# Halving the angle tables of a fused Fourier and mixer kernel's setup, VectorE and ScalarE in step, with masks and identity moved behind the first half

## The chip, the cores and the metric

The kernel runs on one core of a Trainium2 chip. The metric is the device time of one execution in microseconds (us). On one core most executions of the kernel before take 594.2 to 594.5 us. A profile is one execution, and its span is about 1.8 us shorter than the time quoted for it.

TensorE does the matmuls (its weight loads, PEld, run beside them), VectorE (DVE) and ScalarE (ACT) the elementwise work, GpSimd (POOL) issues the loads, SyncE (SP) most of the stores of the result.

## The reference

```python
def reference(x, w_tok1, w_tok2, w_ch1, w_ch2):        # x: 8 x 3008 x 256
    x = fft(fft(x, axis=1), axis=2).real               # Fourier mixing
    h = maximum(x.transpose(0, 2, 1) @ w_tok1, 0) @ w_tok2     # token MLP, 256 hidden
    u = x + h.transpose(0, 2, 1)
    return u + maximum(u @ w_ch1, 0) @ w_ch2           # channel MLP, 1536 hidden
```

## The kernel before

The Fourier transform over 3008 = 64 x 47 positions is made of matmuls with small tables of cosines. The kernel computes these tables itself, in its first 20 us: angles (`mp`), their rounding to whole turns (`vp`), the sine by ScalarE (`tp`, `tq`), then a turn of both tables by TensorE (`pt`, copied to `tt`) and a reversal of their rows with an anti-diagonal matrix (`turn_rows`, `pr`). Meanwhile the first batch is loaded, folded (`xp`), transformed (`pz` to `z`, `pw` to `w`), and carried through the token MLP (`ph`, `pu`, `ut`). At 32 us the first matmul of the channel MLP (`pc`) begins, and from there TensorE works without a pause for 556 us.

The parts that the change touches, cut:

```python
    # head of VectorE
    ts(gt32[:], scol[:], 32.0, AT.is_gt)
    ts(eq32[:], scol[:], 32.0, AT.is_equal)
    ts(mid[:], scol[:], 32.0, AT.is_lt)
    ts(tmp[:], scol[:], 1.0, AT.is_ge)
    nc.vector.tensor_tensor(out=mid[:], in0=mid[:], in1=tmp[:], op=AT.mult)
    # ... reff, offp, gp
    nc.vector.scalar_tensor_tensor(out=mp[:], ...)          # all 12 groups at once
    # ...
    near(vp, mp)                                            # two ScalarE passes of 768
    # ... the small table of z: m1, reduced, sin, t0h
    rest_of(vp, mp, S)
    table3(tp, vp)                                          # two ScalarE passes of 768
    ts(ident[:], jrow[:, 0:P], pcol[:], AT.is_equal)
    # ... vq, anti, t1n, t1b, cfeat/ixc, md

    # the order in which the work is emitted
    warm(24)                            # 24 matmuls that only keep TensorE busy
    table3(tq, vq, (shift0[:], shift1[:]))
    turned_out(tts_p, turn_in(tp, ps_mm))
    filler(12)                          # the same, 128 columns each
    pts_q = turn_in(tq, ps_out)
    filler(4)
    table_d()
    pieces = fold0(); take(pieces, 5)
    own = zw0();      take(own, 2)
    turn_rows(tts_p, 1.0, 0)
    take(own, 3); table_b(); take(own, 3)
    turned_out(tts_q, pts_q)
    # ... three copies of hp, table_perm
    take(own, 4)
    turn_rows(tts_q, -1.0, 0)
    take(own, 3)
    # ...
```

The last batch's result goes out in stores that SP issues, with ScalarE's help, as the last matmuls finish:

```python
                eng = nc.scalar if i and final else nc.sync
                eng.dma_start(
                    out=dram(out_t, (b * S + 8 * c + i + 2 * first) * D,
                             [[NQ * D, 64], [2 * D, nk - first], [1, D]]),
                    in_=osb[64 * i:64 * i + 64, first:nk, :])
```

## Time and profile before

| | kernel before |
|---|---|
| time, median of 3 runs | 594.2 us (594.19 to 594.73) |
| span of the profiled run | 592.44 us |
| TensorE busy | 98% of the span |
| first W product (`pw`) | 18.92 us |
| first matmul of the channel MLP (`pc`) | 32.17 us |
| last TensorE matmul ends | 588.52 us |
| last store landed | 591.14 us |

The lines that carry the prediction are shown in it. How to read them: the page's digits are busy tenths of 40 equal slices; a line of waits gives the engine, what it waited with, what released it, the total in us, how often, and the longest; a line of the chain of waits gives start, length and the work that ended last; a line of the timeline gives start, busy time, engine, source line, operation, tiles out<-in, shapes, count, and in brackets the idle time before it with its releaser.

### The profile page before, as it was taken

To read this page: it belongs to the slowest core of one execution; us is meant where nothing else is said; L and a number is where in the kernel's file an instruction comes from. 1 tells how busy PE (TensorE), PEld (TensorE's weight loads), DVE (VectorE), ACT (ScalarE), POOL (GpSimd) and SP (SyncE) were. 2 spreads that over 40 slices of the span, in tenths; PEclk is the share of its full clock that TensorE was granted. 3 is DMA by queue.
4 is the path that set the end of the run, shared out by engine and by line. 5 is a ranking of instruction groups with operands and counts; after the bars stand their busy time and mean duration, and the time that the engine had idled before them with its cause. 6 is when DMAs were issued, how large, how long until landed. Compare 5 with 4: busy or idle time off the path is not lost.

```text
span 592.4 us, 15959 instructions
## 1 busy us (share of the span) xinstructions
PE 580.4 (98%) x6397; PEld 419.8 (71%) x6397; DVE 458.7 (77%) x1075; ACT 437.7 (74%) x994; POOL 152.7 (26%) x251
## 2 busy tenths in 40 slices
PE   5999999999999999999999999999999999999997
PEld 4846777767776777676777667767777777866676
DVE  8868689878896887769797787868888677676573
ACT  7775887887778777777767776777777867766772
POOL 7530421412151211421134111421211121112131
PEclk9999999999999999999999999999999999999999
DMA  9996851863367242844329432492233335333424
GB/s 151 211 187 126 139 101 46 150 122 54 66 122 139 55 88 56 157 71 98 64 49 170 98 65 55 90 172 54 56 76 63 78 55 97 48 72 72 82 58 105
DMA packets 86683, 56.55 MB, mean 95 GB/s; under 512 B 54945, under 2 KB 83553, under 8 KB 85857
## 3 DMA queue, kind: packets, MB, share of 16 engines
q1 hardware_dynamic: 77984, 37.77, 33.6%
q0 software_dynamic: 8320, 17.49, 17.2%
q8 instruction: 50, 0.82, 0.6%
q10 hardware_dynamic: 304, 0.26, 0.2%
q14 instruction: 25, 0.20, 0.1%
HBM read 34.98 MB, written 24.64 MB: 101 GB/s over the span
## 4 chain that ended last, share of the span: by engine, by line
PE 96%; DVE 2%; ACT 1%; issue 0%; POOL 0%; DVEq 0%; POOLq 0%
PE pc L773 41%; PE px L817 25%; PE py L817 10%; PE pu L730 7%; PE pt L613 4%; PE po L888 2%; PE pz L518 2%; PE pq L645 1%; PE py L645 1%; PE py L836 1%; PE pw L596 1%; PE pw L597 1%; PE pw L560 0%; ACT z L307 0%; PE ph L430 0%; PE ph L432 0%
## 5 line engine op out<-in xcount | busy, mean ns | idle before, releaser
L776 ACT ACTIVATE c<-pc 128x512 f16<-128x512 f32 (+1 forms) x574 | 297.9, 595 | 31.3 <-PE pc L773 16.3
L799 POOL TENSOR_TENSOR osb<-osb,rt 128x256 f32<-128x256 f32 (+1 forms) x92 | 84.5, 919 | 373.3 <-DVE osb L799 366.1
L817 PEld LDWEIGHTS <-c 128*128 128x128 f16 x2112 | 128.1, 98 | 24.9
L773 PE MATMUL pc<-ut,wc1p 128*128 128x512 f16 x576 | 140.0, 379 | 0.5 <-DVE ut L305 0.5
L773 PE MATMUL pc<-ut,wc1m 128*128 128x512 f16 (+1 forms) x576 | 134.9, 370 | 0.0
L822 ACT ACTIVATE m<-px 128x256 f32<-128x256 f32 (+1 forms) x138 | 51.8, 375 | 75.4 <-PE px L817 46.0
L817 PEld LDWEIGHTS <-sb 128*128 128x128 f16 x1584 | 94.6, 98 | 10.4
L738 DVE TENSOR_TENSOR ut<-pu,yt 128x512 f16<-128x512 f32 (+1 forms) x94 | 63.3, 674 | 40.6 <-PE pu L730 40.3
L773 PEld LDWEIGHTS <-wc1p 128*128 128x128 f16 x576 | 52.0, 97 | 49.2 <-DMA wc1p<-in_moe_w_ch_dram,ixc 0.8
L773 PEld LDWEIGHTS <-wc1m 128*128 128x128 f16 x576 | 52.9, 98 | 45.0
L817 PE MATMUL px<-wst,c 128*128 128x128 f16 x1056 | 74.0, 219 | 0.0
L817 PE MATMUL px<-wc,c 128*128 128x128 f16 x1056 | 66.5, 219 | 0.0
L799 DVE TENSOR_TENSOR osb<-py,m 128x256 f32<-128x256 f32 (+1 forms) x92 | 37.5, 407 | 26.5 <-ACT m L822 26.2
L790 DVE TENSOR_TENSOR sb<-sb,c 128x768 f16<-128x768 f16 (+1 forms) x92 | 54.2, 589 | 3.2
L730 PE MATMUL pu<-w2p,uu 128*128 128x512 f16 (+1 forms) x184 | 54.7, 379 | 0.0
L790 DVE TENSOR_TENSOR sb<-c 128x768 f16<-128x768 f16 (+1 forms) x92 | 50.6, 550 | 0.0
L790 DVE TENSOR_TENSOR c<-c 128x768 f16<-128x768 f16 (+1 forms) x92 | 50.5, 548 | 0.0
L790 DVE TENSOR_TENSOR sb<-c,sb 128x768 f16<-128x768 f16 (+1 forms) x92 | 50.4, 548 | 0.0
L307 ACT ACTIVATE z<-pz 128x480 f16<-128x480 f32 (+1 forms) x60 | 39.0, 666 | 5.4 <-PE pz L527 3.0
L599 DVE SCALAR_TENSOR_TENSOR w<-alt,pw 128x131 f16<-128x131 f16 x84 | 29.2, 351 | 16.5 <-ACT w L307 16.0
L652 DVE TENSOR_TENSOR yt<-py,qs 128x512 f16<-128x512 f32 x48 | 30.9, 685 | 10.5 <-ACT qs L648 10.2
L817 PE MATMUL py<-wst,sb 128*128 128x128 f16 x528 | 37.1, 219 | 0.0
(201 smaller groups left out, 648.1 us busy)
## 6 DMA issues: line engine op xcount, KB each, us to landing
out_dram<-osb SPq DMA_DIRECT2D x83, 256.0 KB, 3.8
xp<-in_x_dram POOLq DMA_DIRECT2D x16, 272.0 KB, 5.3
out_dram<-osb SPq DMA_DIRECT2D x11, 192.0 KB, 3.1
xp<-in_x_dram POOLq DMA_DIRECT2D x16, 127.5 KB, 5.8
rt<-ut SPq DMA_TRANSPOSE x96, 3.8
w2s<-in_moe_w_tok_dram POOLq DMA_DIRECT2D x1, 1504.0 KB, 14.8
w1p<-in_moe_w_tok_dram POOLq DMA_DIRECT2D x4, 192.0 KB, 7.9
wc<-in_moe_w_ch_dram POOLq DMA_DIRECT2D x1, 768.0 KB, 15.2
```

The lines of the kernel that those rows point to most:

```text
L307: nc.scalar.activation(out=out_, in_=in_, func=AFT.Copy)
L599: nc.vector.scalar_tensor_tensor(out=w[:, g, 0:131], in0=alt[:], scalar=pw[:, 131:132], in1=pw[:, 0:131], op0=AT.mult, op1=AT.add)
L613: nc.tensor.matmul(pt[:, o:o + n], lhsT=hw[:, g, th * P:th * P + P], rhs=w[:, g, f:f + n], start=(g == 0), stop=(g == NG - 1))
L652: nc.vector.tensor_tensor(out=yt[:, h, CW * c:CW * c + CW], in0=py[:], in1=qs[:], op=op)
L730: nc.tensor.matmul(pu[:, 0:n], lhsT=uu[:, th, int(minus), h, :], rhs=w2_cols(b, c)[:, th], start=(th == 0), stop=(th == 1))
L738: nc.vector.tensor_tensor(out=ut[:, h, 0:n].rearrange("p (a b) -> p a b", b=64), in0=pu[:, 0:n].rearrange("p (b a) -> p a b", b=64), in1=y ...
L773: nc.tensor.matmul(pc[:, 0:n], lhsT=wc[:, h, ct * P:(ct + 1) * P], rhs=ut[:, h, 0:n], start=(h == 0), stop=(h == 1))
L776: nc.scalar.activation(out=c1[:, ct, 0:n], in_=pc[:, 0:n], func=AFT.Relu)
L790: nc.vector.tensor_tensor(out=o, in0=x, in1=y, op=op)
L799: eng.tensor_tensor(out=o, in0=x, in1=y, op=AT.add)
L817: nc.tensor.matmul(o[:, t], lhsT=a(k)[:, f:f + P], rhs=w(k), start=(first and t == 0 and k == 0), stop=(k == HC - 1), skip_group_check=True)
L822: nc.scalar.activation(out=m[:, i, t1], in_=pa[:, 0], func=AFT.Copy)
```

## The change

Its intent: the chain that ends last in the setup goes through one large VectorE instruction, two large ScalarE passes, another VectorE one, and so on, each waiting for the whole of the one before. In halves of six groups the two engines can work side by side. Work that is not needed early (the masks `mid`, the small table of z, the identity) moves behind the first half; the turned rows of p move ahead of the z products; the index of the gathered weights is made by GpSimd. The diff's core, cut:

```diff
-    ts(mid[:], scol[:], 32.0, AT.is_lt)
-    ts(tmp[:], scol[:], 1.0, AT.is_ge)
-    nc.vector.tensor_tensor(out=mid[:], in0=mid[:], in1=tmp[:], op=AT.mult)
...
+    halves = slice(0, NG // 2), slice(NG // 2, NG)
+    for g in halves:
+        nc.vector.scalar_tensor_tensor(out=mp[:, g], ...)
+    ts(mid[:], ...)                       # the three of mid, moved here
+    for g in halves:
+        for i, scale, bias in ((mp, 1.0 / S, up), (vp, 1.0, down)):
+            nc.scalar.activation(out=vp[:, g], in_=i[:, g], func=AFT.Identity,
+                                 scale=scale, bias=bias[:])
+    rest_of(halves[0])
     half = pvec("half0"), pvec("half1")
     ...
+    rest_of(halves[1])
+    ident = const.tile([P, P], FP16, tag="ident")
+    ts(ident[:], jrow[:, 0:P], pcol[:], AT.is_equal)
     quart, side, shift0, shift1 = ...
+    for g in halves:
+        table3(tp, vp, g)
...
-    cfeat = pvec("cfeat")                 # three VectorE instructions for ixc
+        iota(ixc[:], [[0, 1]], D, -1)     # by GpSimd
...
-    Z0_ORDER = ((11, (0, 0)), (0, (1, 1)), (6, (0, 1)), (1, (0, 1)))
+    Z0_ORDER = ((11, (0, 1)), (0, (1, 1)), (6, (0, 1)), (1, (0, 1)))
...
-    warm(24)
-    table3(tq, vq, (shift0[:], shift1[:]))
-    turned_out(tts_p, turn_in(tp, ps_mm))
-    filler(12)
+    warm(12)
+    pts_p = turn_in(tp, ps_mm)
+    turned_out(tts_p, pts_p, (0,))
+    angles_z()
+    turned_out(tts_p, pts_p, (1,))
+    table_q()
+    table_anti()
+    table_z()
+    filler(6)
+    turn_rows(tts_p, 1.0, 0)
+    filler(10)
     pts_q = turn_in(tq, ps_out)
     filler(4)
...
```

Note the fillers. Before there are 24 + 12 + 4 = 40 matmuls that compute nothing, after it 12 + 6 + 10 + 4 = 32. Each comes with a weight load, so TensorE has 16 instructions fewer, and all else it does is the same.

More of the change, by code (lines that the diff above doesn't have):

```diff
@@ L248, in sin, with table3 @@
         nc.scalar.activation(out=out_, in_=in_, func=AFT.Sin, scale=PI2 / period)
-    def table3(tab, r, shift=(0.0, 0.0)):
+    def table3(tab, r, g, shift=(0.0, 0.0)):
         for i in range(2):
-            nc.scalar.activation(out=tab[:, :, 64 * i:64 * i + 64], in_=r[:],
+            nc.scalar.activation(out=tab[:, g, 64 * i:64 * i + 64], in_=r[:, g],
                                  func=AFT.Sin, scale=half[i][:], bias=shift[i])
@@ L268, in turn_in, with turned_out @@
         return pts
-    def turned_out(tts, pts):
-        for h in range(2):
+    def turned_out(tts, pts, hs=(0, 1)):
+        for h in hs:
             copy(0, tts[0][:, 768 * h:768 * h + 768], pts[h][:, 0:768])
@@ L318 @@
     ts(gp[:], jrow[:, 0:NG], r2[:], AT.mult, offp[:], AT.add)
-    nc.vector.scalar_tensor_tensor(
-        out=mp[:], in0=jrow[:, 0:64].unsqueeze(1).to_broadcast([P, NG, 64]),
-        scalar=r47[:], in1=gp[:].unsqueeze(2).to_broadcast([P, NG, 64]),
-        op0=AT.mult, op1=AT.add)
+    halves = slice(0, NG // 2), slice(NG // 2, NG)
+    for g in halves:
+        nc.vector.scalar_tensor_tensor(
+            out=mp[:, g], in0=jrow[:, 0:64].unsqueeze(1).to_broadcast([P, NG // 2, 64]),
+            scalar=r47[:], in1=gp[:, g].unsqueeze(2).to_broadcast([P, NG // 2, 64]),
+            op0=AT.mult, op1=AT.add)
+    ts(mid[:], scol[:], 32.0, AT.is_lt)
+    ts(tmp[:], scol[:], 1.0, AT.is_ge)
+    nc.vector.tensor_tensor(out=mid[:], in0=mid[:], in1=tmp[:], op=AT.mult)
     nc.vector.memset(altu[:], 1.0)
@@ L325, with rest_of @@
         nc.vector.memset(altu[:, f:f + 127:2], -1.0)
-    def near(v, m):
-        for i, scale, bias in ((m, 1.0 / S, up), (v, 1.0, down)):
-            nc.scalar.activation(out=v[:], in_=i[:], func=AFT.Identity, scale=scale,
-                                 bias=bias[:])
-    def rest_of(v, m, period):
-        nc.vector.scalar_tensor_tensor(out=v[:], in0=v[:], scalar=-float(period),
-                                       in1=m[:], op0=AT.mult, op1=AT.add)
-    near(vp, mp)
+    for g in halves:
+        for i, scale, bias in ((mp, 1.0 / S, up), (vp, 1.0, down)):
+            nc.scalar.activation(out=vp[:, g], in_=i[:, g], func=AFT.Identity,
+                                 scale=scale, bias=bias[:])
+    def rest_of(g):
+        nc.vector.scalar_tensor_tensor(out=vp[:, g], in0=vp[:, g], scalar=-float(S),
+                                       in1=mp[:, g], op0=AT.mult, op1=AT.add)
+    rest_of(halves[0])
     half = pvec("half0"), pvec("half1")
@@ L345, with table_q, table_anti @@
                                        op0=AT.mult, op1=AT.mult)
+    for g in halves:
+        table3(tp, vp, g)
+    anti = const.tile([P, P], FP16, tag="anti")
+    acol = pvec("acol")
+    def table_q():
+        for g in halves:
+            nc.vector.scalar_tensor_tensor(out=vq[:, g], in0=vp[:, g], scalar=side[:],
+                                           in1=vp[:, g], op0=AT.mult, op1=AT.max)
+        for g in halves:
+            table3(tq, vq, g, (shift0[:], shift1[:]))
+    def table_anti():
+        ts(acol[:], pcol[:], -1.0, AT.mult, 127.0, AT.add)
+        ts(anti[:], jrow[:, 0:P], acol[:], AT.is_equal)
     mask0, mask0h, q24 = (pvec(n) for n in ("mask0", "mask0h", "q24"))
-    ts(mask0h[:], xicol[:], -0.5, AT.mult, 0.5, AT.add)
-    ts(q24[:], qcol[:], 24.0, AT.add)
     t1n = const.tile([KR, 2, 2, 24], FP16, tag="t1n")
@@ L351 @@
     m1 = gen.tile([KR, 5, 24], FP32, tag="m1")
-    for a, n, col, off in ((0, 2, qcol, 47 / 4), (2, 2, qcol, 0.0), (4, 1, q24, 47 / 8)):
-        ts(m1[:, a:a + n, :], jrow[0:KR, 0:24].unsqueeze(1).to_broadcast([KR, n, 24]),
-           col[0:KR, :], AT.mult, off, AT.add)
     cs, v1 = (gen.tile([KR, 5, 24], FP32, tag=n, name=n) for n in ("cs", "v1"))
-    reduced(v1[:], m1[:], m1[:], 47)
-    sin(cs[:], m1[:], 47)
     t0h = gen.tile([KR, 2, 24], FP16, tag="t0h")
-    nc.scalar.activation(out=t0h[:], in_=cs[:, 0:4:2, :], func=AFT.Copy,
-                         scale=mask0h[0:KR, :])
@@ L361 @@
-    rest_of(vp, mp, S)
-    table3(tp, vp)
-    ident = const.tile([P, P], FP16, tag="ident")
-    ts(ident[:], jrow[:, 0:P], pcol[:], AT.is_equal)
-    nc.vector.scalar_tensor_tensor(out=vq[:], in0=vp[:], scalar=side[:], in1=vp[:],
-                                   op0=AT.mult, op1=AT.max)
-    anti = const.tile([P, P], FP16, tag="anti")
-    acol = pvec("acol")
-    ts(acol[:], pcol[:], -1.0, AT.mult, 127.0, AT.add)
-    ts(anti[:], jrow[:, 0:P], acol[:], AT.is_equal)
-    ts(mask0[:], mask0h[:], 2.0, AT.mult)
@@ L372, with angles_z @@
-    for i, m in ((0, mask0), (1, xicol)):
-        ts(t1n[:, :, i, :], cs[:, i:4:2, :], m[0:KR, :], AT.mult)
-    ts(t1b[:, 1, :], cs[:, 4, :], float(np.sqrt(0.5)), AT.mult,
-       xicol[0:KR, :], AT.mult)
-    nc.vector.tensor_copy(out=t1b[:, 0:3:2, :], in_=t1n[:, :, 0, :])
+    def angles_z():
+        ts(mask0h[:], xicol[:], -0.5, AT.mult, 0.5, AT.add)
+        ts(q24[:], qcol[:], 24.0, AT.add)
+        for a, n, col, off in ((0, 2, qcol, 47 / 4), (2, 2, qcol, 0.0),
+                               (4, 1, q24, 47 / 8)):
+            ts(m1[:, a:a + n, :], jrow[0:KR, 0:24].unsqueeze(1).to_broadcast([KR, n, 24]),
+               col[0:KR, :], AT.mult, off, AT.add)
+        reduced(v1[:], m1[:], m1[:], 47)
+        sin(cs[:], m1[:], 47)
+        nc.scalar.activation(out=t0h[:], in_=cs[:, 0:4:2, :], func=AFT.Copy,
+                             scale=mask0h[0:KR, :])
@@ L377, with table_z @@
+    def table_z():
+        ts(mask0[:], mask0h[:], 2.0, AT.mult)
+        for i, m in ((0, mask0), (1, xicol)):
+            ts(t1n[:, :, i, :], cs[:, i:4:2, :], m[0:KR, :], AT.mult)
+        ts(t1b[:, 1, :], cs[:, 4, :], float(np.sqrt(0.5)), AT.mult,
+           xicol[0:KR, :], AT.mult)
+        nc.vector.tensor_copy(out=t1b[:, 0:3:2, :], in_=t1n[:, :, 0, :])
     nyq = const.tile([KR, P], FP16, tag="nyq")
     ixc = const.tile([P, 1], I32, tag="ixc")
-    cfeat = pvec("cfeat")
-    ts(cfeat[:], pcol[:], 1.0, AT.is_lt, -128.0, AT.mult)
@@ L381, with rows_c, angles_d @@
-    ts(cfeat[:], cfeat[:], 256.0, AT.add)
-    nc.vector.tensor_tensor(out=ixc[:], in0=cfeat[:], in1=pcol[:], op=AT.subtract)
-    nc.vector.scalar_tensor_tensor(out=md[:], in0=vd[:], scalar=-256.0, in1=md[:],
-                                   op0=AT.mult, op1=AT.add)
+    def rows_c():
+        iota(ixc[:], [[0, 1]], D, -1)
+        pl.memset(ixc[0:1, :], P)
+        load_wc()
+    def angles_d():
+        nc.vector.scalar_tensor_tensor(out=md[:], in0=vd[:], scalar=-256.0, in1=md[:],
+                                       op0=AT.mult, op1=AT.add)
@@ L387 @@
     alt = const.tile([P, 131], FP16, tag="alt")
-    load_wc()
     def table_d():
@@ L932, in take @@
             next(g, None)
-    warm(24)
-    table3(tq, vq, (shift0[:], shift1[:]))
+    warm(12)
     held.add("o2")
-    turned_out(tts_p, turn_in(tp, ps_mm))
-    filler(12)
+    pts_p = turn_in(tp, ps_mm)
[8 more added lines that the diff above has]
+    filler(10)
     pts_q = turn_in(tq, ps_out)
     filler(4)
-    table_d()
+    rows_c()
     pieces = fold0()
-    take(pieces, 5)
+    take(pieces, 2)
+    angles_d()
+    take(pieces, 3)
     own = zw0()
     take(own, 2)
-    turn_rows(tts_p, 1.0, 0)
+    turned_out(tts_q, pts_q, (0,))
     take(own, 3)
+    turned_out(tts_q, pts_q, (1,))
+    held.clear()
+    take(own, 3)
+    table_d()
     table_b()
-    take(own, 3)
-    turned_out(tts_q, pts_q)
-    held.clear()
-    for g2, e in enumerate((1, 1, 0)):
-        carried(tts_p, hp, g2, e)
+    carried(tts_p, hp, 0, 0)
+    carried(tts_p, hp, 1, 1)
+    turn_rows(tts_q, -1.0, 0)
+    carried(tts_p, hp, 2, 1)
     table_perm()
-    take(own, 4)
-    turn_rows(tts_q, -1.0, 0)
-    take(own, 3)
+    take(own, 7)
     carried(tts_p, hp, 3, 1)
```

## The prediction

> **What bounds the kernel now.** I read the page first, for the share of each engine and the clock:
>
> ```profile
> PE 580.4 (98%) x6397; PEld 419.8 (71%) x6397; DVE 458.7 (77%) x1075; ACT 437.7 (74%) x994; POOL 152.7 (26%) x251
> ...
> PE   5999999999999999999999999999999999999997
> ...
> PE 96%; DVE 2%; ACT 1%; issue 0%; POOL 0%; DVEq 0%; POOLq 0%
> ```
>
> TensorE is the bound, and the only slice with room is the first (its digit is 5). The whole table of waits of TensorE over the span says the same:
>
> ```profile
> PE filler L294 <- DVE altu L325: 5.9, 1, 5.9
> PE pz L518 <- ACT tt L287: 0.6, 1, 0.6
> PE pc L773 <- DVE ut L305: 0.5, 1, 0.5
> PE pw L560 <- ACT tt L307: 0.4, 1, 0.4
> PE pz L518 <- DVE xp L488: 0.4, 1, 0.4
> PE pt L265 <- ACT tq L252: 0.3, 1, 0.3
> ```
>
> All six fall before 32.2 us. From the first matmul of the first MLP layer (`pc`) to the end, TensorE never waits. The matmuls after it are the same in both kernels, so the question is only: at what time does that first `pc` start? The chain of waits, cut to its first 42 us, shows who sets that time (start, length, what):
>
> ```profile
> 4.26 1.02 DVE mp L319
> ...
> 8.09 0.87 DVE vp L333
> ...
> 12.16 0.77 DVE xp L488 x2
> ...
> 14.50 1.08 ACT z L307 x2
> 15.58 1.45 ACT tt L287 x3
> ...
> 18.92 1.09 PE pw L560 x16
> ```
>
> VectorE leads up to 13.4 us almost without a hole, ScalarE from 14.5 to 18.9, then TensorE is fed back to back from 18.92 to about 31.4. That is the chain which the change works on. But there is a second arm, which the chain does not show because it ended a tenth of a microsecond earlier. The weight loads' waits and the timeline around 32 us:
>
> ```profile
> PEld L773 <- DMA wc1p<-in_moe_w_ch_dram,ixc: 0.8, 1, 0.8
> ...
> 31.42 0.69 DVE L305 CAST ut<-pu 128x512 f16<-128x512 f32 x1 [1.16 <-PE pu L716]
> ...
> 32.17 1.46 PE L773 MATMUL pc<-ut,wc1p 128*128 128x512 f16 x6 [0.52 <-DVE ut L305]
> ```
>
> and the DMA issue of the same weights, from the timeline and from the list of issues:
>
> ```profile
> 15.79 1.05 POOL L153 DMA_INDIRECT wc1p<-in_moe_w_ch_dram,ixc  x1 [0.96 <-DVE xp L488]
> ...
> wc1p<-in_moe_w_ch_dram,ixc POOLq DMA_INDIRECT x1, 16.2
> ```
>
> 15.79 + 16.2 = 31.99 us: the gathered half of the first layer's weights lands at 31.99, and the weight loads wait for it. `ut`, the end of the compute chain, is there at 31.42 + 0.69 = 32.11. So two arms end within 0.12 us of one another. The second matmul of `pc` (start 32.38 in the trace) is the first that needs the gathered half. The DMA view has the engines at 9 tenths in nearly every slice from 4 us on, at some 195 to 215 GB/s; landings come in the order of issue (w1 by 20.26, w2s 28.21, the direct half of the weights 30.07, the gathered half 31.99). That arm is bandwidth and order, not issue: the gather lay 16 us in the queue.
>
> **What the Trainium skill says.** "DMA: Bandwidth & Descriptors", section "Issuing engines are not separate DMA queues", and the skill's main page "Trainium Kernel Development and Optimization", Key Constraints: all queues share the same 16 DMA engines. Here one queue carries nearly everything, and the trace agrees: an earlier issue behind a full queue gains nothing by itself. "ScalarE: Activation LUTs", section "What ACT_TABLE_LOAD costs": an ACTIVATE costs a fixed part plus 0.833 ns per element. The trace agrees: 255 elements took 0.507 us and 768 took 0.936, so 0.836 ns per element and 0.29 us fixed; that fixed part, less some overlap, is what each split pays. "TensorE: Matmul & The Clock Gate", Part 1: the array runs at half rate until some 3.4 us of sustained activity. The trace agrees: the fillers of 256 columns start at 5.89 and stand 0.213 us apart, and the spacing falls only at about 10.5 us; the transposes of 128 columns from 10.9 on stand 0.056 us apart.
>
> **The change, part by part.** The order of the instructions on each engine in both programs was compared, since the engines run in order.
>
> *The head of VectorE.* The three `mid` instructions leave the head; `reff` starts after `gt`/`eq`, 0.26 us earlier (2.58 for 2.84), so `mp` may start at 4.01. Halved, it takes about 0.59 us a half (estimate: 1.02 less 384 elements at the 0.99 ns per element that the 259- and 512-wide casts, 0.42 and 0.67 us, give, and with overlap), so ScalarE starts on `vp` at 4.60 instead of 5.32: 0.7 us earlier.
>
> *ScalarE.* The rounding is four passes of 384 at about 0.615 us (0.29 + 384 x 0.836 ns) in sequence with two overlaps of 0.1: 4.60 to 7.03, against 7.22 before. `sin`/`t0h` of the small table (0.3 + 0.34) no longer stand ahead of the `tp` table, and `tp` starts at about 6.95 and not 8.99. Its four passes end near 9.1 instead of 10.75: 1.6 us earlier. Then TensorE turns `tp`: the 12 warm matmuls end at 5.89 + 12 x 0.213 = 8.45, the transposes run at half rate (12 x 0.107 = 1.3 us), so the last is in at about 9.9, and `tt` follows half by half, ending near 11.4 instead of 13.98. `tq` (four passes, about 0.6 us apart) then ends near 13.7; it ended at 12.59 before: later, by design. `turn_rows` of p moves ahead to about 13.7-15.3 from 15.47-17.04.
>
> *VectorE up to the fold.* Gone: three `cfeat`/`ixc` instructions (0.45 us; made by GpSimd now). Moved behind the fold's first pieces: `md` (0.42). Added: three splits, about 0.12 us each, and a new idle of about 0.5 us, as the second half of `rest_of` needs ScalarE's fourth pass (7.03) while VectorE is free at 6.6. Saved at the head, after moving `mid` back in: nothing. Net: the fold starts at about 12.3 (12.16 before), and with `md` in it ends near 15.7 (15.31).
>
> *After the fold.* One `z` copy of 480 columns moves from ScalarE to VectorE (0.68 us, from the 0.63 to 0.82 us of its like). VectorE: 15.7 + 0.68 + two small z copies (0.65) + two large (1.3) = 18.4. ScalarE: from `turn_rows` at 15.2: three z copies (0.5 + 0.55 + 0.63), two `tt` of q (0.69 each), the two `sin` of `tdu` (0.5) = 18.7. Both arms meet in `tdb`, at about 19.2; before, `pw` started at 18.92. In step, as intended, but not earlier.
>
> *What then is gained.* `turn_rows` of q (three matmuls, 0.65 us of TensorE at 19.85-20.5) now lies ahead of the first `pw`, in time that TensorE spends waiting. So TensorE's back-to-back stretch is 0.65 shorter and starts 0.3 later: -0.35 us. Against it stands VectorE: from `tdb` on it has two hp copies, nine w copies and one more hp (3 x 0.6 + 9 x 0.34 = 4.9 us) before the last w: 19.2 + 4.9 = 24.1, and the matmul that needs all of w ran at 24.07. This eats the gain. Compute arm in sum: -0.35 to +0.1, say -0.1 us.
>
> *The DMA arm.* Not one transfer is removed, shrunk or moved ahead of the gather; only its index is ready sooner. The gather is issued near 15.1 instead of 15.8, into a queue that is 16 us deep. It lands at 31.99 again, give or take 0.1.
>
> The start of the `pc` stream is the later of the two arms. If compute came much earlier, the gain would stop where the second `pc` matmul waits for the gather: 32.38 - 32.0 = 0.38 us at the most.
>
> **The rivals.** (1) *The weights' DMA takes the place of the wait.* For it: 31.99 against 32.11, and the 0.8 us wait of the weight loads. Against: nothing. It caps the gain at 0.38 us: 593.8 at best. (2) *VectorE is the bound from 12 to 24 us and is given more to do.* For it: busy 2.88 of 3 us from 16 to 19; the z copy of 0.68 and the splits. Against: turn_rows out of the way. It would make `ut` 0.3 to 0.6 later: 594.5 to 594.8. (3) *TensorE stays or falls back to half rate*, with 12 instead of 24 warm matmuls and a hole of about 1 us until `anti` is made at about 11.4. For it: the rate rose at 10.5 only after 4.6 us of unbroken work. Against: before, the stretch from 14 to 16 had 1.42 of 2 us busy and the rate held. It would cost 0.5 to 1 us or more. (4) *The plan works wholly*, compute ends 0.7 us earlier: then rival 1 holds it at 593.8.
>
> **Range and chances.** Most likely -0.1 us, so 594.1. Downwards the DMA closes the range at about 593.8, with 0.2 for the scatter of landings; upwards rivals 2 and 3, and the scatter of the three runs before (594.19 to 594.73), give 594.9. 2% are 11.9 us; the whole stretch in which anything changes holds 2.2 us of TensorE waits after its first matmul (0.6 + 0.5 + 0.4 + 0.4 + 0.3) and 32 us in all. So 98% within 2%, and 1% for each side.
>
> **What would show it.** In the profile after: `tp` ends near 9.1; the fold on VectorE starts at about 12.2 to 12.4; the first `pw` at about 19.2 with no turned rows behind it; the gather lands at 31.9 to 32.1; the first `pc` between 31.4 and 32.6, and the second not before 32.0, followed by no wait of TensorE. The prediction is wrong if the gather lands clearly earlier than 31.8 (then the DMA arm is not bandwidth alone), if the matmuls after 11 us stand 0.107 us apart (half rate), if `ut` comes after 32.7, or if TensorE waits anywhere after 33 us.

## The result, and the profile after

The changed kernel took 595.38 us in the median of 4 runs (594.62, 595.34, 595.80, 595.42), the kernel before 594.22 (594.19 to 594.73) in the same rounds. The ratio of the two is 1.0013, 95% interval 0.9998 to 1.0028; it is computed, here and below, as the mean time of one kernel's fast runs over that of the other's of the same rounds, so it is not quite the ratio of the medians. Within 2%, as predicted, but 0.5 us above the top of the predicted range, and in the wrong direction (an interval that reaches from just below 1 does not by itself prove a loss; experiment 1 repeats it). The profiled run is the one of 594.62, 0.4 us above the kernel before.

The page of the changed kernel, the lines that answer to those of before:

```profile
PE 579.1 (98%) x6389; PEld 418.7 (71%) x6389; DVE 459.5 (78%) x1076; ACT 438.5 (74%) x999; POOL 153.2 (26%) x253
...
PE   4999999999999999999999999999999999999997
...
PE 96%; DVE 3%; ACT 0%; issue 0%; POOL 0%; DVEq 0%; POOLq 0%
```

TensorE has 8 matmuls and 8 weight loads fewer (6389 for 6397), all of them filler, and is busy 1.3 us less. Its table of waits over the whole span:

```profile
PE filler L291 <- DVE altu L327: 6.1, 1, 6.1
PE pr L278 <- DVE mask L97: 1.4, 1, 1.4
PE pt L262 <- ACT tq L249: 0.7, 1, 0.7
PE pc L792 <- DVE ut L302: 0.5, 1, 0.5
PE pz L537 <- ACT tt L304: 0.5, 1, 0.5
```

Again every wait is over by 32.3 us. The wait of `pw` and one of the two of `pz` are gone. `pr` waits 1.4 us for the anti-diagonal matrix and `pt` 0.7 instead of 0.3, both where TensorE has nothing urgent. The chain of waits, cut to its first 33 us:

```profile
4.01 0.63 DVE mp L318
...
7.11 0.56 DVE vp L335
...
12.31 0.27 issue
12.59 0.77 DVE xp L507 x2
...
16.07 2.67 DVE z L302 x5
...
18.96 0.31 DVE tdb L417
19.31 0.56 PE pw L579 x7
...
32.30 0.81 PE pc L792 x3
```

What was ScalarE's share of the chain from 14.5 to 18.9 is VectorE's now. The first `pc` stands at 32.30 instead of 32.17. And the weights' arm, from the weight loads' waits, where the row of before was also 0.8:

```profile
PEld L792 <- DMA wc1p<-in_moe_w_ch_dram,ixc: 0.8, 1, 0.8
```

Nothing has changed there. So the setup as a whole costs 0.13 us at the first `pc` and 0.07 us at the last TensorE matmul, which ends at 588.59 for 588.52. But the span is 0.40 longer. The other 0.33 us arise after the last matmuls. The timeline of SP (SPq is its sequencer, and the busy time is that of issuing a store), of the kernel before, for the last stores of the last but one chunk and the group of the last one:

```profile
585.56 0.62 SPq L858 DMA_DIRECT2D out_dram<-osb  x1
586.43 2.94 SPq L912 DMA_DIRECT2D out_dram<-osb  x3
```

and of the changed kernel:

```profile
585.63 1.27 SPq L877 DMA_DIRECT2D out_dram<-osb  x1
587.00 2.44 SPq L931 DMA_DIRECT2D out_dram<-osb  x3
```

The second store of the pair took 1.27 us to issue instead of 0.62, and the next could begin only at 587.00 instead of 586.43. What was different at 585.6? The DMA view of 580 to 593 us, GB/s in 40 slices of 0.325 us, of the kernel before:

```profile
GB/s 0 0 0 0 0 0 0 0 0 0 0 0 0 50 0 0 0 0 3 189 198 192 148 227 293 252 240 214 280 337 256 199 199 0 0 0 0 0 0 0
```

and of the changed kernel:

```profile
GB/s 0 0 0 0 0 0 0 0 0 0 0 0 0 0 0 50 0 0 0 139 189 205 186 230 195 192 183 196 170 249 363 344 255 133 0 0 0 0 0 0
```

The lone 50 is one packet of 16 KB on the queue that both pages list as "q8 instruction": 50 packets in the run. It lies two slices later after the change: it starts at 584.27 before and at 585.06 after, counted in the trace, and so falls just ahead of the store issue of 585.63. Some 12,800 TensorE instructions for 50 fetches are 256 instructions each; and the last fetch starts when TensorE has begun 12,708 instructions before, 12,706 after (matmuls, loads, and 11 of its sequencer). A stream that is 16 instructions shorter reaches that count 16 instructions closer to its end, which at the 21 to 22 instructions per us of this stretch is 0.75 us later (an estimate from the windows of both traces; measured 0.79).

### The profile page after: what moved, and what is told of

Its sections match the earlier page's. It is cut to its first block, busy times and chain, and to the rows that moved or that the text cites. A ratio compares the mean times of both kernels' runs of the same rounds, so it can differ in the third digit from the quotient of the medians.

```text
span 592.8 us, 15951 instructions
## 1 busy us (share of the span) xinstructions
PE 579.1 (98%) x6389; PEld 418.7 (71%) x6389; DVE 459.5 (78%) x1076; ACT 438.5 (74%) x999; POOL 153.2 (26%) x253
## 4 chain that ended last, share of the span: by engine, by line
PE 96%; DVE 3%; ACT 0%; issue 0%; POOL 0%; DVEq 0%; POOLq 0%
PE pc L792 41%; PE px L836 25%; PE py L836 10%; PE pu L749 7%; PE pt L632 4%; PE po L907 2%; PE pz L537 2%; PE pq L664 1%; PE py L664 1%; PE py L855 1%; PE pw L615 1%; PE pw L616 1%; PE pw L579 1%; DVE z L302 0%; DVE xp L507 0%; ACT vp L331 0%
```

## The experiments

Four theories stood against each other. Where an expectation uses a letter: A is a TensorE that runs at half rate in part of the setup, because 24 warm matmuls became 12 with a hole behind them (rival 3 of the prediction), thought of at first as a fall back and later as a full clock that comes late; B is that the order of the changed setup itself ends later, at whichever engine; C is that the TensorE instruction count moves the last instruction fetch onto a store issue; D, found on the way, is that the loads of the first batch come late in some executions. The order is that in which they ran; the theories were sharpened between them.

**1. The changed kernel unaltered, 5 more rounds.** No edit.

> The changed kernel unaltered, five timed rounds. In the four runs so far it gave 594.62 (mean granted clock 1.000) and 595.34, 595.80, 595.42 (0.999, 0.997, 0.998). Theory A (in some runs the TensorE clock falls back to half rate once in the setup, because of the new holes in TensorE's work): two kinds of runs again, one near 594.6 with a granted clock of 0.999 to 1.000 and one 0.7 to 1.3 us longer at 0.997 to 0.998, median 595 to 595.6. Theory B (the compute arm is simply 0.1 to 0.5 us longer on VectorE and the rest is scatter): one cloud around 594.6 to 595, no tie to the clock.

Measured: 594.91 us (594.62 to 595.02) against 594.23 (9 runs, 594.19 to 594.36), ratio 1.0011, 0.9997 to 1.0024. The interval still holds 1, but all five runs lie above all nine of the kernel before. So I take the loss as real, close to 0.7 us on this chip and not 1.2. It is the single cloud that theory B expected; the trace shows that most of it is not lost in the setup. Trace: first `pc` 32.31, end of the last matmul 588.60, span 593.06. The issue at 585.64 took 1.46 us, with the fetch at 585.25, and a second one was long too:

```profile
587.89 1.24 SPq L931 DMA_DIRECT2D out_dram<-osb  x1
```

Of the 0.62 us of span over the kernel before, 0.08 lie ahead of the end of the last matmul and 0.54 behind it.

**2. Fill the hole in TensorE's work.**

```diff
-    filler(6)
+    filler(30)
```

> The changed kernel with 30 instead of 6 filler matmuls between the transposes of tp and the turned rows: at 0.056 us each, 24 more fill 1.34 us of the 1.38 us hole that TensorE has from 10.2 to 11.58. Theory A: the longer runs vanish or get rare, median 594.4 to 594.7, spread below 0.6. Theory B: nothing changes, median as e1.

Measured: 594.27 (four runs 594.22 to 594.32, one of 595.35), ratio 1.0005. First `pc` 32.30 as in the changed kernel, yet the time is that of the kernel before. Read alone it speaks for theory A, for it closes the hole; but the full clock had come at 11.36, later than the 9.47 of the changed kernel's own trace, so the clock was not what it mended. It also adds 48 TensorE instructions: the last fetch lies at 584.35 and no issue at the end is long.

**3. Make the holes in the kernel before.**

```diff
-    filler(12)
+    filler(1)
     pts_q = turn_in(tq, ps_out)
-    filler(4)
+    filler(1)
```

> The kernel before with its own fillers cut (12 to 1 after the transposes of tp, 4 to 1 after those of tq), so that TensorE has holes of about 1.1 and 0.8 us from 11.5 to 14.1, nothing else changed. Theory A: it gets the longer runs too, median 594.8 to 595.6 or at least one run in five 0.7 us or more above 594.3. Theory B: 594.2 as before.

Measured: 594.82 (594.28, 594.82, 594.86, 594.79, 594.96), ratio 1.001. I first took this for support of A. The trace says otherwise: the full clock came at 11.90 and stayed, first `pc` 32.25, but 28 instructions fewer put the fetch at 585.96, and the issue at 586.56 took 1.61 us. In that traced run it cost nothing (594.28); why that one run escaped is open. Holes and instruction count are mixed in this edit, so it decides nothing.

**4. Make the anti-diagonal matrix first, which removes most of the hole.**

```diff
-    table_q()
     table_anti()
+    table_q()
```

> The changed kernel with the mirror matrix made before vq instead of after it: the hole of 1.38 us on TensorE is cut in two (the first turned row can go at about 10.5, the other two at about 11.6), the order on ScalarE stays. vq moves back by 0.35 us, which still is ready before ScalarE wants it. Theory A: fewer long runs than e1, median 594.4 to 595.0. Theory B: as e1 within 0.2 us.

Measured: 594.69 (594.53 to 594.96), ratio 1.0007. `pr` waits 0.6 us instead of 1.4 and starts at 10.53 for 11.58; the first `pc` gains 0.02, the time keeps its loss, and the issues at 585.61 and 587.96 are long (1.55 and 1.25). The median, 0.2 us below that of experiment 1, fits the range of theory A as well; the trace speaks against A, for with most of the hole gone 0.70 us are lost behind the last matmul. The hole is not the cause of that loss; experiment 6 shows the same from the other side.

**5. The kernel before with 16 TensorE instructions fewer in the same TensorE time.** Twelve fillers of 128 columns become four of 384.

```diff
+    def wide(n):
+        pw = ps_any("filler")
+        for _ in range(n):
+            nc.tensor.matmul(pw[:, 0:384], lhsT=ident[:],
+                             rhs=tp[:, 0:3, :].rearrange("p a b -> p (a b)"),
+                             start=True, stop=True)
...
-    filler(12)
+    wide(4)
```

> The kernel before, its 12 fillers of 128 columns after the transposes of tp made into 4 of 384: the same TensorE time and no new hole, but 16 instructions fewer on TensorE, as many as the changed kernel has fewer. Theory A (holes let the clock fall back): 594.2, as before. Theory B (the longer compute arm): 594.2. Theory C (the instruction fetch of 16 KB, which comes once per some 256 TensorE instructions, moves from 584.3 to about 585.1 us and so falls onto the issue of the output stores at 585.6 us, which then takes 1.2 to 1.5 us instead of 0.62 and lands later): 594.6 to 595.0 in most runs, with that issue over 1.1 us in the trace, first pc still at 32.17.

Measured: 594.73 (594.46 to 594.83, one run of 596.29) against 594.29 for the kernel before on this chip (11 runs, 594.18 to 595.68), ratio 1.0008. The setup did not suffer: first `pc` 32.14, end of the last matmul 588.52. The fetch moved to 585.05, and the issue behind it is the long one of the changed kernel:

```profile
585.55 1.26 SPq L865 DMA_DIRECT2D out_dram<-osb  x1
```

Span 592.80, 0.36 over the kernel before. This is the change's loss at the end, made without the change.

**6. The changed kernel with 16 instructions more, its hole left in place.** Ten fillers of 128 columns become 18 of 71: 1278 columns for 1280.

```diff
-    def filler(n):
+    def filler(n, w=P):
...
-    filler(10)
+    filler(18, 71)
```

> The changed kernel with its 10 fillers of 128 columns made into 18 of 71: the same TensorE time, the hole of 1.38 us stays, but 16 instructions more on TensorE, so as many as the kernel before has. Theory A: as the changed kernel, 594.6 to 595.0. Theory B: as the changed kernel. Theory C: the last fetch back at about 584.3, no store's issue over 0.75 us at the end, 594.2 to 594.4 in most runs; first pc still at 32.3.

Measured: 594.37 (594.23, 594.37, 594.24, and two of 594.95 and 595.37), ratio 1.0003. Trace: first `pc` 32.25, end of the last matmul 588.55, span 592.46, fetch at 584.35, and

```profile
585.59 0.62 SPq L877 DMA_DIRECT2D out_dram<-osb  x1
```

Runs 5 and 6 make and undo the loss at the end by the instruction count alone, each in one trace and in the median of its runs. Theory C holds. (The two long runs of this experiment were not traced.)

**7. One z copy back from VectorE to ScalarE.**

```diff
-    Z0_ORDER = ((11, (0, 1)), ...
+    Z0_ORDER = ((11, (0, 0)), ...
```

> The changed kernel with the z copy that it moved to VectorE (0.65 us) back on ScalarE. The number of TensorE instructions is that of the changed kernel. If VectorE alone sets the start of pc, pc comes 0.3 to 0.6 earlier, up to the landing of the gathered weights at 32.0; if the two are in step (both free at 18.7), ScalarE's sines come 0.5 later and pc starts at 32.4 to 32.8. Theory C: the end of the last store and the time follow the tail as in the changed kernel, 594.6 to 595.4.

Measured: 595.13 (594.89, 595.15, 596.01, 595.11), ratio 1.0015, 1.0000 to 1.0029. Both sines that `tdu` needs come later, and VectorE stands idle for them:

```profile
18.88 0.22 DVE L99 TENSOR_SCALAR tdu<-tdu 128x1 f16<-128x1 f16 x2 [0.72 <-ACT tdu L245]
```

The first `pw` is at 19.25 for 19.00, the first `pc` at 32.53 for 32.30. (The second, at 33.01, waited for weights that were late in that execution, so I count 0.23 us and not more.) The two engines are in step: in the changed kernel's chain VectorE leads up to `tdb`, and with this copy on ScalarE it is ScalarE that leads. Behind the last matmul this trace lost nothing (3.92 us to the end of the span, as in the kernel before), though the fetch was at 585.65 and the issue at 586.14 took 0.97 us; the tail that I had expected did not come.

**8. Shorten the compute arm of the changed kernel.** The first batch skips half of the token MLP's first product; its result is wrong.

```diff
-            for g in range(NG):
+            step = 1 if b else 2
+            for g in range(0, NG, step):
```

> Wrong result on purpose: the changed kernel with half of the products of the first token matmul of the first sample left out (24 matmuls of 0.056 us, 1.35 us), so that the compute arm ends near 30.9. This measures the DMA arm by itself. If the weights' gather caps the gain as predicted: the first pc (direct half) starts near 31.0, the second waits for the gather and starts at 31.9 to 32.1, so the stream gains at most 0.4 to 0.6 of the 1.35 us. If the DMA follows the compute: the second pc starts near 31.2.

Measured: 595.12, one look. Meant for the weights' arm, it fell into theory A's state by chance, so it decides nothing on the weights. The timeline of TensorE, though, shows the late clock, in a setup that is the changed kernel's own:

```profile
8.61 1.49 PE L262 MATMUL pt<-ident,tp 128*128 128x128 f16 x12
...
13.88 1.49 PE L262 MATMUL pt<-ident,tq 128*128 128x128 f16 x12
```

Twelve transposes in 1.49 us both times, at 13.9 still at half rate. Full rate came at 15.35 and the first `pw` at 19.61, 0.6 us late. So A exists, in some executions. The time holds something else too: the last matmul ended only 0.21 us later than in the kernel before, and 0.70 us were lost behind it, where ScalarE's last store issue, at 589.09, took 1.17 us, with the last fetch at 588.93.

**9. Provoke the late clock.**

```diff
-    warm(12)
+    warm(2)
...
-    filler(6)
+    filler(1)
```

> The changed kernel with 2 instead of 12 warm matmuls and 1 instead of 6 fillers before the turned rows, so that TensorE has too little work to be given full rate before some 14 to 15.5 us; this makes the late rate, which one trace of the changed setup (with a short arm) showed by chance at 15.35 us, happen on purpose. If the late rate is what the long runs have (595.3 to 595.8): spacing of transposes 0.107 us until after 13 us, first pw at 19.5 to 19.8 instead of 19.0, first pc at 33.0 to 33.5 instead of 32.3, median 595.0 to 596.0. If the rate in the setup does not matter: pc at 32.3 to 32.5.

Measured: 595.73 (595.32 to 595.88), ratio 1.0016, 1.0001 to 1.0032. Full rate at 15.65, first `pw` 19.79, first `pc` 32.94. A late clock costs 0.6 us at the first `pc`. Its loads were late as well, by 1.5 us, but TensorE shows no wait for them. It has 30 instructions fewer still, and the issue at 588.45 took 1.16 us, so the time holds a part of C too.

**10. The changed kernel with its instruction count restored by eight more fillers.**

```diff
-    filler(6)
+    filler(14)
```

> The changed kernel with 14 instead of 6 fillers in the hole: 16 instructions more on TensorE, as many as the kernel before has, and a third of the hole filled. Theory C with the late rate: tail as before (last fetch near 584.3, no long issue), median 594.25 to 594.40 with fewer long runs; what remains over 594.23 is the compute arm, 0.1. Otherwise as the changed kernel, 594.6 or more.

Measured: 594.39 (594.22 to 594.48), against 594.26 for the kernel before on this chip (9 runs, of which three of 595.48 to 595.55), ratio 0.9993; those three make the ratio look better than it should. Six of the nine runs lie at 594.18 to 594.40, so the repaired kernel is about 0.1 us behind an undisturbed kernel before: about what its first `pc`, 32.30, says. In its trace the last fetch came at 584.88, 0.75 us ahead of the issue at 585.63, and that issue took 0.62 us: a fetch near a store issue does not always lengthen it.

**11. A version that mends both costs.** VectorE's idle 0.47 us ahead of the second `rest_of` is filled with the work that stands behind it, three warm matmuls go, and fillers bring the TensorE instructions back to the count before.

```diff
-    rest_of(halves[1])
     ident = const.tile([P, P], FP16, tag="ident")
     ...
     # quart, side, shift0, shift1
+    rest_of(halves[1])
...
-    warm(12)
+    warm(9)
...
-    filler(6)
+    filler(17)
```

> An attempt at a better version: the changed kernel with the identity and the shift columns put ahead of the second half of the rest (VectorE waits 0.47 us for ScalarE there), 9 instead of 12 warm matmuls (the first transposes wait for them until 8.62, their table half is ready at 8.1) and 17 instead of 6 fillers, which restores TensorE's count of before. Expected: VectorE and ScalarE 0.3 to 0.45 us earlier, pw at 18.5 to 18.7, first pc at 31.8 to 32.0, second pc held by the gather at 31.95 to 32.2; time 593.9 to 594.15, if the clock is not late. If VectorE's idle time only moves, 594.25 to 594.4.

Measured: 594.04 (593.98, 593.98, 594.04, 594.25, and the traced run, 594.87), ratio 0.9989, 0.9975 to 1.0002. The trace caught a state not seen before, theory D: the loads of the first batch came 0.9 us late (second half of w1 issued at 13.27 for 12.38), TensorE waited 0.4 us for them and then 0.4 us for w, and the first `pc` was at 32.91. The issue time alone does not tell this state: in experiment 4 that load was issued at 13.27 too, and no wait followed.

**12. Shorten the compute arm of the kernel before.** The edit of experiment 8, in the kernel before. Its output is wrong, which doesn't matter for the time.

> Wrong result on purpose: the kernel before with half of the products of the first token matmul of the first sample left out (24 matmuls of 0.056 us). Repeats the measurement of the DMA arm, which the late clock spoilt in the first attempt. If the gather caps the gain: first pc at 30.8 to 31.1, second pc not before 31.9 to 32.1, so its stream comes 0.3 to 0.45 earlier than 32.38 though the arm is 1.35 shorter. If not: second pc at about 31.1.

Measured: 594.62, one look. The edit takes 24 matmuls of 0.056 us, 1.35 us, out of the arm. A new wait of 0.87 us for hq ate most of it. The timeline of TensorE, and that of its weight loads:

```profile
31.82 1.47 PE L774 MATMUL pc<-ut,wc1p 128*128 128x512 f16 x6 [0.52 <-DVE ut L305]
```

```profile
32.03 0.76 PEld L774 LDWEIGHTS <-wc1p 128*128 128x128 f16 x5 [1.06 <-DMA wc1p<-in_moe_w_ch_dram,ixc]
```

0.35 us arrive at the first `pc`, 31.82 for 32.17, and at the second, 32.04 for 32.38. But the load of the gathered weights, which in the kernel before began together with the first `pc`, now begins 0.21 us behind it: it waits for the gather, and the second `pc` starts as soon as it is there. So at a gain of 0.35 us the two arms meet, near the cap of 0.38 that rival 1 gave; that a larger gain would be lost was not tried. The last matmul ended at 588.21, 0.32 us earlier, and still the run took 0.4 us longer. Two issues at 587.42, one by SP and one by ScalarE, took 1.08 and 1.13 us: 48 TensorE instructions fewer had put the fetch at 587.67.

**Four looks, to see the state of the long runs.** Three traced executions of the changed kernel and one of the kernel before, on a fourth chip, after the twelve experiments. No edit.

> The changed kernel unaltered, one traced execution, to see in which state its longer runs are. If it takes 594.6 to 595.0, the first MLP matmul should stand at 32.3 and a store issue of 1.1 to 1.6 us near 585.6. If it takes 595.3 to 595.8, either the full clock comes only after 14 us (transposes 0.107 us apart, first W product at about 19.6, first MLP matmul at 33.0: late clock), or the second half of w1 is issued near 13.2 instead of 12.4 and TensorE waits for it, first MLP matmul near 32.9 (late loads).

> As look1_after, a second traced execution of the changed kernel: 594.6 to 595.0 with the first MLP matmul at 32.3 and a long store issue near 585.6, or 595.3 to 595.8 with either the late clock (full rate after 14 us, first MLP matmul near 33.0) or the late loads (second half of w1 issued near 13.2, first MLP matmul near 32.9).

> The same changed kernel a third time, traced: 594.6 to 595.0 with the first MLP matmul at 32.3 and a long store issue near 585.6; or 595.3 to 595.8 with the late clock (first MLP matmul near 33.0, full rate after 14 us) or the late loads (second half of w1 issued near 13.2).

> The kernel before, traced on the same chip: 594.2 with the first MLP matmul at 32.17 and no store issue over 1 us after 584 us; or its own long state of 595.4 to 595.7, in which case I expect late loads (second half of w1 issued about 0.9 us late, TensorE waiting for it), not a late clock, because its fillers keep TensorE busy.

Measured: 595.07, 595.14, 594.58 and 594.22. The kernel before was as always (first `pc` 32.16, no issue over 0.75 us after 584 us). The run of 594.58 is like the first trace: `pc` 32.26, one long issue of 1.27 us. The two of 595.1 showed neither of the expected pictures in pure form, but late loads in part and two long issues. From the GpSimd timeline and the weight loads' waits of the first:

```profile
14.17 0.64 POOL L173 DMA_DIRECT2D w1m<-in_moe_w_tok_dram  x1 [1.42 <-DMA xm<-in_x_dram,ix]
```

```profile
PEld L451 <- DMA w1m<-in_moe_w_tok_dram: 0.4, 1, 0.4
```

This load is issued at 12.4 to 12.9 in most traces; it waits for the gathered rows of x, which landed at 13.88 for 12.19. The last matmul ended 0.27 us later than before's, and the two issues (1.51 and 1.23) cost 0.58 us after it: together the 0.86 by which the span is longer.

**The version of experiment 11 again**, on a fifth chip.

> The version of e11 once more, on another chip and traced in what I hope is its undisturbed state. If its gain is real: median 593.9 to 594.2, the ratio's interval at or below 1.000, first MLP matmul near 31.9 to 32.1, the gather landing at 32.0 and gating the second one (not before 32.2), no store issue over 1 us after 584 us. If e11's low times were luck of one chip: 594.2 to 594.4, first MLP matmul at 32.2 to 32.3.

Measured: 594.03 (593.98 to 594.23) against 594.34 (9 runs, 594.18 to 595.79), ratio 0.999, 0.9976 to 1.0004. This time the traced run was undisturbed, and both repairs are to be seen in the timelines of TensorE and SP:

```profile
32.08 1.46 PE L792 MATMUL pc<-ut,wc1p 128*128 128x512 f16 x6 [0.52 <-DVE ut L302]
```

```profile
585.40 0.62 SPq L877 DMA_DIRECT2D out_dram<-osb  x1
```

The second `pc` stands at 32.29, close to the landing of the gather in this trace (32.19). The last matmul ended at 588.36, 0.16 us earlier than before's. On both chips the undisturbed runs lie at 594.0, against 594.2 for those of the kernel before: a gain of 0.2 us, smaller than the intervals of the ratios, which just reach above 1 because they count the long runs of the kernel before.

## Why the prediction was wrong, step by step

*The head.* Right. `mp` at 4.01, the chain's second `rest_of` with its new idle of 0.47 (predicted 0.5), `tp` done at 9.10 (9.1). ScalarE's four passes of rounding ended at 7.07 for 7.03, though the sum as written, 4.60 + 4 x 0.615 less two overlaps of 0.1, gives 6.86.

*VectorE up to the fold and behind it.* Nearly right. The fold began at 12.59 for 12.3; the 0.27 us "issue" ahead of it, which the sum did not have, is that difference. The terms that the prediction lists add up to 12.15, not 12.3 (12.16 - 0.45 - 0.42 + 0.36 + 0.5), and its end of the fold, 15.7, fits only the former; it ended at 16.07. `tdb` ended at 19.26 (19.2), the last w at 24.06 (24.1).

*The compute arm in sum.* The sign was wrong: -0.1 predicted inside "-0.35 to +0.1", +0.13 measured at the first `pc`, just outside. This is the prediction's rival 2 in a small size: the chain and experiment 7 show that neither VectorE nor ScalarE had room there.

*The DMA arm.* Right in the result: in the one trace of the changed kernel that recorded it undisturbed, the gather landed at 32.05 (31.9 to 32.1 predicted), though it was issued at 15.72 and not near 15.1, and in experiment 12 the two arms met after 0.35 us. But the row of 0.8 us, which the prediction took as evidence, proves little: in both kernels that weight load begins together with the first `pc`, so `ut` ended that wait, and the name in the row is only the latest release that the profile knew of.

*The late clock, rival 3.* Real, but rare: one trace of an unaltered setup has it (experiment 8), none of the five traces of the changed kernel itself. The cost of 0.6 us fits the "0.5 to 1 us or more". The prediction says that the trace agrees with some 3.4 us of work at half rate; its own figures, 5.89 to 10.5, are 4.6 us, and the point moves from run to run (last section).

*What failed* is the step in the first part: "The matmuls after it are the same in both kernels, so the question is only: at what time does that first `pc` start?" and with it the range, which allowed for nothing at the end of the kernel and took the scatter of the kernel before for that of the changed one. It left out a second path to the end of the run: the last stores. The matmuls after it are the same, but they stand 16 instructions earlier in TensorE's stream. That shifts the last instruction fetch by 0.79 us onto a store issue that nothing hides any more. Behind the last matmul it costs 0.33 to 0.36 us in the three traces with one long issue at 585.6 (the first, the third look, experiment 5), 0.54 to 0.70 in the four with two. Experiments 5 and 6 show this cause both ways. The sum for a typical run of the changed kernel on the chip of experiment 1: 594.2 + 0.1 for the setup + 0.5 for the end = 594.8, measured 594.9. That is the top of the predicted range, so this step explains most of the typical loss, but not the whole of the first result, 595.4.

*What stays open.* The fetch that falls on a store does not always cost: in the traced runs of experiments 3 and 7 it cost nothing. Over all chips, the twelve unaltered runs of the changed kernel have a median of 595.0. The rest up to the 595.3 to 595.8 of three of its first four runs was never traced: late loads with two long issues gave 595.1, and with the 0.6 us of a stronger delay, as in experiment 11, or of a late clock, they would give 595.5 to 595.7, but this is argued and not shown. The kernel before has long runs of 595.4 to 595.8 too, on three of four chips with nine or more runs (2 of 9, 2 of 11, 3 of 9, 0 of 9), also untraced. What makes the gathered rows of x land late was not found. Nor was the reason why a second issue, near 588, takes 1.24 us: it came in all four traces of the changed order in which the first took 1.46 us or more, and in none of those with 1.27, and no fetch lies near it.

## What to carry to other kernels

When a stretch of a tuned kernel is rebuilt, look at the end as well as at the stretch: an edit that only removes filler matmuls moved the instruction fetches of all that follows, and the last stores, which nothing hides, paid for it. Where tenths of a microsecond matter, keep the number of TensorE instructions while the order is changed, or choose it so that the last fetch does not meet the last stores; eight dummy matmuls more (experiment 10) won back about half a microsecond. And trace several executions before believing one: two of the theories here were states that only some executions have.

## What the Trainium skill lacked or had wrong

- No page has the slow store issue; it would belong to "DMA: Bandwidth & Descriptors". Over 19 traces, from 60 us on, a store issued by SP from 0.5 us before to 1 us after the start of a 16 KB instruction fetch took more than 0.9 us in 77 of 293 cases (up to 1.9), elsewhere in 4 of 1,569; the median elsewhere is 0.6 us. Of the 77, 66 lie ahead of 580 us, where no TensorE wait follows. Those four of the 1,569 are the second long issues named above. ScalarE's issues beside the last fetch took 1.13 to 1.21 us in experiments 8, 9 and 12. How a fetch slows an issue no run shows.
- No page says at which instruction of the stream a fetch comes. "Runtime: NRT & Kernel Launch", section "Instruction fetch mechanics", has only its size, 16 KiB or 256 instructions, with which the 50 fetches for some 12,800 TensorE instructions agree. Over 19 traces of thirteen kernels the last one started when TensorE had begun 12,706 to 12,751 instructions. A spread of 45 is about 2 us at 21 to 22 a us (an estimate from these traces), so the count alone does not place a fetch exactly.
- "TensorE: Matmul & The Clock Gate", Part 1, puts the change to full rate around 4 us into sustained work, within 0.5 us from run to run. The runs agree that it varies, but here it varied more: full rate came 2.7 (experiment 7) to 6.0 us (experiment 3) after the first matmul, and after 9.3 and 9.6 us in experiments 8 and 9, where TensorE had holes of over 1 us in its work, at a cost of 0.6 us. Holes alone do not bring it: the changed kernel has one of 1.4 us too. What places the change no run shows.
